# Two-layer network behind local attention: the first 512 features of layer one join the planned order, its weights are scaled, and the additions of its seven-product inputs are split between two engines

## The chip, the cores and the metric

The kernel runs on one core of a Trainium2 chip. TensorE (PE, with PEld for its weight loads) multiplies, VectorE (DVE), ScalarE (ACT) and GpSimd (POOL) do the elementwise work, and SyncE (SP) issues most of the transfers. Every engine works through a queue of its own in order and waits on semaphores for the others. The metric is the device time of one execution in microseconds (us).

## The reference

```python
x = attention(q, k, v)              # B=2, H=8, S=768, D=64: window of 16, and 24 block summaries
x = x.transpose(0, 2, 1, 3).reshape(1536, 512)
h = x @ moe_w_in                    # 512 x 2048
x = (h * np.cos(h)) @ moe_w_out     # 2048 x 512
h = x @ moe2_w_in
return (h * np.tanh(np.log1p(np.exp(h)))) @ moe2_w_out
```

Scores are masked outside a window of 16 positions; each query also sees 24 summaries of 32 keys (maximum) and values (mean). The weights arrive as 64-bit numbers.

## The kernel before

**Products.** A value is kept as a high part (fp32r) and a low part (value minus high part), and a product is three passes: high by high, high by low, low by high. Tokens come in three blocks of 512; hidden features in pieces of 128. So one product of 128 features by 512 tokens over the 512 inputs is 12 matmuls, and ends in one of eight PSUM banks.

**Attention** comes first: 48 steps of 128 tokens, software pipelined, all emitted through one `flush` (L280). Its result is `X`, a high and a low tile (`xh`, `xl`). Between its steps the first weights of layer one are made ready: a chunk is loaded, narrowed to 32 bits (`wnarrow`, L142 to L154, DVE, four instructions of which the long path takes three on DVE), and split (`whole`: high on ACT at L167, low at L172). For the first 512 features of layer one the low is on POOL, eight chunks of 128x512: four of `w_in`, four of `w_out`.

**Layer one, first 512 features.** A loop over 12 tiles (3 token blocks by 4 pieces of features) runs `up(k)` (L208, 12 matmuls into bank k modulo 4) and, one tile behind, the gate h cos h: whole turns on ACT (L589), two subtractions of them on DVE (L590 reads PSUM, L591 reads SBUF alone), the sine on ACT (L595), the product on DVE (`cos_gate`, L597, which reads the bank for the last time), then the high part on ACT (L582) and the low on DVE (L583). A tile can begin only when the tile four before has had its L597. `down` (L613) multiplies the gates with `w_out`, its evictions are on ACT (L615). The first three tiles' matmuls are fillers of attention's last steps.

**Layer one, the rest, and layer two.** The other features come in halves of 256. There seven products of sums take the place of eight (`prod`, L749), with input sums T1 to T4 that are made once from `X`: 16 additions (`tpiece`, all on POOL, emitted through `sub`, L643) and eight splits (`tsplit`). The work of these halves is placed by a planner, `arrange()`: each operation has an engine (A, D, P, S), a length in steps of six matmuls, dependencies and a due step, and it is emitted at the begin the planner finds for it. Only the order in each engine's queue comes from the plan; no wait does. At the seam, layer two's first features (`pe1` L915, then `pe2` L927) are interleaved with the last halves of layer one, and DVE there adds the last downs to `acc`, makes layer two's input sums and narrows its weights. Layer two (L1223) is emitted by a loop again.

Of the kernel before, what the change touches and what calls it, by code (L numbers as in the profile page):

```python
# [21 lines left out]
def kernel(  # L22
# [36 lines left out]
    C1 = 6.28125  # L59
    C2 = TWO_PI - C1  # L60
# [13 lines left out]
    b_floor = const.tile([128, 1], F32, tag="b_floor", name="b_floor")  # L74

# [488 lines left out]
    def layers():  # L564
        with ExitStack() as es:
# [5 lines left out]
            gate = [8, 9] + [n % 8 for n in range(200)]  # L571
# [6 lines left out]

            def split(g):

                hi, lo = gslot()
                nc.scalar.copy(hi, g)  # L582
                nc.vector.tensor_tensor(out=lo, in0=g, in1=hi.bitcast(F32), op=ALU.subtract)  # L583
                return hi, lo

            def turns(h):

                n, r = tmp("n", 2, I32), tmp("r")
                nc.scalar.activation(out=n, in_=h, func=AF.Identity, scale=1.0 / TWO_PI, bias=b_quarter)  # L589
                nc.vector.scalar_tensor_tensor(out=r, in0=n, scalar=-C1, in1=h, op0=ALU.mult, op1=ALU.add)  # L590
                nc.vector.scalar_tensor_tensor(out=r, in0=n, scalar=-C2, in1=r, op0=ALU.mult, op1=ALU.add)  # L591
                return h, r

            def cos_gate(h, r):
                nc.scalar.activation(out=r, in_=r, func=AF.Sin, bias=b_hpi)  # L595
                g = tmp("gg")
                nc.vector.tensor_tensor(out=g, in0=r, in1=h, op=ALU.mult)  # L597
                return g
# [8 lines left out]
            def down(s, u, bank=None):  # L607
                l, g, j = stages[s]
                ps = (dbank() if bank is None else BANK[bank])[:, 0:TB]
                mm = [(SLOT[4 * (g % 2) + 2 + a][:, 512 * f + 128 * u:512 * f + 128 * u + 128], G[s, f][e])  # L610
# [3 lines left out]
                acc = ACC[l, j][:, TB * u:TB * u + TB]  # L614
                return lambda: nc.scalar.copy(acc, ps)  # L615

            downs, adds = [], []

            def do_adds():
                while adds:  # L620
                    adds.pop(0)()

            def do_downs(k):

                for _ in range(2):
                    if downs and downs[0][0] <= k:
                        adds.append(down(*downs.pop(0)[1:]))

            def made(k, i, g):

                s, f = G_OF = tiles[i]
                G[G_OF] = g
                if f == GF - 1:
                    late = 2 if s == 0 else 1
                    downs.extend((k + late + u, s, u) for u in range(KD))

# [12 lines left out]
            def tpiece(p, i):  # L649
# [8 lines left out]
                sub(out, u, v, op, nc.gpsimd)  # L658

            def tsplit(p, i, part):  # L660
# [7 lines left out]
                else:  # L668
                    sub(lo, f, hi.bitcast(F32))

            TSEQ = {}

            def tseq(k, op, *a):
                TSEQ.setdefault(k, []).append((op, *a))

            for p in range(2):
                for i in range(8):
                    tseq(5 + p + (i > 5), 1, p, i)
                for i, (k0, k1) in enumerate(((7, 7), (8, 8), (10, 11), (9, 10))):
                    tseq(k0 + (p if i < 2 else 0), 0, p, i, 0)  # L680
                    tseq(k1 + (p if i < 2 else 0), 0, p, i, 1)

            st = {}
            NT1 = len(tiles)
            for k in range(NT1):
                if k not in HP:
                    up(k)
                h = HP.pop(k)
                g = cos_gate(*st.pop(k - 1)) if k - 1 in st else None
                do_adds()  # L690
                st[k] = turns(h)
                if g is not None:
                    made(k, k - 1, split(g))
                for op in WSEQ.get(k, ()):
                    op()
                for op, *arg in TSEQ.get(k, ()):
                    (tpiece if op else tsplit)(*arg)
                do_downs(k)

# [84 lines left out]
            BY = {"A": nc.scalar, "D": nc.vector, "P": nc.gpsimd}  # L784
# [13 lines left out]
            def arrange():  # L798
# [27 lines left out]
                free = {}  # L826
                left = list(ops)
# [533 lines left out]
```

## Time and profile before

| what | us |
|---|---|
| three runs: lowest, median, highest | 625.95, 626.74, 627.63 |
| the profiled execution, its own time | 626.33 |
| its span in the trace | 624.6 |
| PE busy in the span | 612.4 (98%) |
| DVE / ACT / POOL busy | 507.8 / 373.9 / 184.8 |

The span begins with the first instruction that the profile shows and ends with the last; 1.73 us of the execution lie outside it. In 40 slices of 15.6 us PE is at nine tenths or more in all but two: the ninth (125 to 140 us, seven tenths) and the last (eight tenths). The chain of work that ended last runs over PE for 88% of the span.

### The profile page before, as it was taken

The numbers are of one execution on the slowest core, as the hardware profiler recorded it, in microseconds if no ns is written. First come the engines' busy times: TensorE is split into PE (matmuls) and PEld (weight loads), VectorE is DVE, ScalarE is ACT, GpSimd is POOL, SyncE is SP. The second block draws the span as 40 slices with busy tenths as digits, with TensorE's granted clock in tenths as the row PEclk, the third lists the DMA queues.
The fourth block names the chain that finished last, engine by engine and source line by source line (L and its number), as shares of the span: only waits on it lengthen the run. The fifth ranks groups of instructions, "written<-read, shape, count | busy, mean of one in ns | idle before, by whom it ended". The sixth has DMA issues, their size and how long they took to land.

```text
span 624.6 us, 8840 instructions
## 1 busy us (share of the span) xinstructions
PE 612.4 (98%) x3012; PEld 499.1 (80%) x3013; DVE 507.8 (81%) x1002; ACT 373.9 (60%) x783; POOL 184.8 (30%) x263
## 2 busy tenths in 40 slices
PE   9999999979999999999999999999999999999998
PEld 4787778758888888888888887888888888888886
DVE  4698995599896888888988999678898888888653
ACT  4699897448977675757576767563444444444230
POOL 4599977692042333333330362000000000000000
PEclk9999999989999999999999999999999999999999
DMA  9879842002213222222223220112021213130005
GB/s 189 199 181 234 173 111 69 2 0 68 65 70 101 68 68 68 68 68 68 68 68 101 69 68 1 41 42 87 35 101 35 102 34 102 34 102 34 1 17 186
DMA packets 57995, 49.88 MB, mean 80 GB/s; under 512 B 44270, under 2 KB 44526, under 8 KB 57710
## 3 DMA queue, kind: packets, MB, share of 16 engines
q1 hardware_dynamic: 57950, 49.32, 28.1%
q8 instruction: 24, 0.39, 0.3%
q14 instruction: 21, 0.17, 0.1%
HBM read 45.57 MB, written 3.15 MB: 78 GB/s over the span
## 4 chain that ended last, share of the span: by engine, by line
PE 88%; DVE 9%; issue 1%; ACT 1%; POOL 0%; ACTq 0%; POOLq 0%
PE bank L749 32%; PE bank L1223 19%; PE bank L280 14%; PE bank L915 13%; PE bank L613 5%; PE bank L208 3%; PE bank L927 2%; DVE acc L643 2%; DVE gl L583 1%; DVE r L591 1%; DVE gl L643 1%; DVE r L590 1%; DVE wx L148 0%; DVE wx L154 0%; DVE wx L151 0%
## 5 line engine op out<-in xcount | busy, mean ns | idle before, releaser
L749 PE MATMUL bank<-xh,ws 128*128 128x512 f32 x464 | 156.5, 389 | 0.0
L1223 PE MATMUL bank<-ws,gh 128*128 128x512 f32 (+1 forms) x356 | 108.6, 387 | 0.0
L749 PEld LDWEIGHTS bank<-xh,ws 128*128 128x128 f32 x464 | 87.1, 188 | 18.1
L915 PE MATMUL bank<-gh,ws 128*128 128x512 f32 x288 | 95.2, 389 | 0.0
L749 PE MATMUL bank<-xl,ws 128*128 128x512 f32 x232 | 90.3, 389 | 0.0
L1223 PEld LDWEIGHTS bank<-ws,gh 128*128 128x128 f32 x356 | 66.6, 188 | 13.7
L167 ACT CAST ws<-wx 128x512 fp32r<-128x512 f32 x66 | 40.1, 619 | 52.4 <-DVE wx L154 49.7
L1223 PE MATMUL bank<-ws,gl 128*128 128x512 f32 (+1 forms) x178 | 68.8, 387 | 0.0
L915 PEld LDWEIGHTS bank<-gh,ws 128*128 128x128 f32 x288 | 54.1, 188 | 11.3
L280 POOL TENSOR_TENSOR pn<-pb,rs 128x256 f32<-128x256 f32 (+3 forms) x120 | 55.4, 483 | 18.1 <-ACT pb L280 6.2
L915 PE MATMUL bank<-gl,ws 128*128 128x512 f32 x144 | 56.0, 389 | 0.0
L1235 DVE TENSOR_TENSOR acc<-acc,bank 128x512 f32<-128x512 f32 (+1 forms) x71 | 47.5, 674 | 8.5 <-PE bank L1223 8.5
L719 DVE TENSOR_TENSOR gl<-gg,gh 128x512 fp32r<-128x512 f32 x42 | 29.1, 692 | 28.5 <-ACT gh L718 28.5
L749 PEld LDWEIGHTS bank<-xl,ws 128*128 128x128 f32 x232 | 43.5, 188 | 9.0
L725 ACT ACTIVATE gg<-gg 128x512 f32<-128x512 f32 x28 | 17.7, 633 | 51.2 <-DVE gg L724 51.2
L643 DVE TENSOR_TENSOR acc<-acc,bank 128x512 f32<-128x512 f32 x62 | 42.2, 682 | 4.2 <-PE bank L915 3.3
L188 POOL TENSOR_TENSOR wx<-wx 128x256 f32<-128x256 f32 x24 | 22.6, 940 | 76.6 <-DVE ws L174 75.3
L280 ACT ACTIVATE pb<-pb,mx 128x182 f32<-128x182 f32 x96 | 42.3, 448 | 1.1 <-DVE mx L280 0.9
L643 POOL TENSOR_TENSOR gl<-gg,gh 128x512 fp32r<-128x512 f32 x18 | 24.6, 1367 | 59.0 <-ACT gh L891 44.1
L749 PE MATMUL bank<-ws,ws 128*128 128x512 f32 x156 | 39.6, 389 | 0.0
L1223 PEld LDWEIGHTS bank<-ws,gl 128*128 128x128 f32 x178 | 33.4, 188 | 6.8
L172 DVE TENSOR_TENSOR ws<-wx,ws 128x512 fp32r<-128x512 f32 x48 | 33.4, 710 | 5.7 <-ACT ws L167 4.5
(139 smaller groups left out, 1315.9 us busy)
## 6 DMA issues: line engine op xcount, KB each, us to landing
wst<-in_moe_w_in_dram SPq DMA_DIRECT2D x32, 512.0 KB
wst<-in_moe_w_out_dram SPq DMA_DIRECT2D x32, 512.0 KB
kn<-in_k_dram SPq DMA_DIRECT2D x16, 192.0 KB
qn<-in_q_dram SPq DMA_DIRECT2D x16, 192.0 KB
vn<-in_v_dram SPq DMA_DIRECT2D x16, 192.0 KB
out_dram<-acc SPq DMA_DIRECT2D x11, 256.0 KB
vb<-in_v_dram SPq DMA_DIRECT2D x2, 960.0 KB
vt<-in_v_dram SPq DMA_DIRECT2D x32, 18.8 KB
```

The lines of the kernel that those rows point to most:

```text
L167: nc.scalar.copy(hi, x)
L172: eng.tensor_tensor(out=lo, in0=x, in1=hi.bitcast(F32), op=ALU.subtract)
L188: (nc.vector if l else nc.gpsimd).tensor_tensor(out=z, in0=u, in1=v, op=op)
L208: nc.tensor.matmul(ps, lhsT=SLOT[4 * (g % 2) + a][:, 512 * c + 128 * f:512 * c + 128 * f + 128], rhs=X[e][:, c, TB * j:TB * j + TB], start ...
L280: todo[phase].append(lambda: fn(*a, **kw))
L613: nc.tensor.matmul(ps, lhsT=x, rhs=y, start=(n == 0), stop=(n == len(mm) - 1))
L643: (eng or nc.vector).tensor_tensor(out=out, in0=x, in1=y, op=op)
L719: later.append(lambda: nc.vector.tensor_tensor(out=lo, in0=g, in1=hi.bitcast(F32), op=ALU.subtract))
L749: nc.tensor.matmul(ps, lhsT=u, rhs=v, start=start and n == 0, stop=stop and n == len(mm) - 1)
L915: nc.tensor.matmul(BANK[bank], lhsT=x, rhs=y, start=(n == 0 and (h == HF or not stay)), stop=(n == len(mm) - 1 and (h == NH - 1 or not stay)))
L1223: nc.tensor.matmul(ps, lhsT=x, rhs=y, start=(n == 0 and (h == 0 or not stay)), stop=(n == len(mm) - 1 and (h == NH - 1 or not stay)))
L1235: nc.vector.tensor_tensor(out=acc, in0=acc, in1=ps, op=ALU.add)
```

## The change

1. The twelve tiles of the first 512 features are put in the planner, gates and evictions too: up to T7 first, then two of the first block's downs, and so on. The hand-written loop and its tables are gone. A gate takes three DVE instructions instead of four: `rest` (whole turns off, reads a bank), `times` (reads a bank), and the low. For that `w_in` of these features carries a factor of 1/(2 pi), folded into the split in attention; for those four chunks the low is now a DVE instruction with the factor, and narrowing takes two DVE instructions instead of three for all eight chunks.
2. The 16 additions are planned no earlier than behind tile T5; eight go to POOL (all that read `X` alone), eight to DVE; of the eight low parts four to POOL.
3. The planner gets an engine "V": a VectorE operation with all operands in SBUF. It and a POOL operation exclude each other in the plan ("share"). POOL's planned length falls from 1.04 to 0.95, and a due step at the end of the planned part is not enforced any more.
4. A one-column sine at the second step after attention's last scores loads ACT's table there.
5. Evictions of the first block's downs alternate between ACT and DVE. In the last half of layer one, downs and layer two's first products are interleaved differently.

PE's list has as many rows as before (2151), SP's is the same. DVE's goes from 966 to 954, POOL's from 233 to 222.

```diff
     def short(l, g, c):
-        return (l == 0 and g > 0) or (l, g) == (1, 0) or (l, g, c) in ((1, 1, 2), (1, 1, 3))
+        return l == 0 or (l, g) == (1, 0) or (l, g, c) in ((1, 1, 2), (1, 1, 3))
...
         if fast:
-            if part == 1:
+            if part == 1 and (l, g) == (0, 0):
+                nc.vector.tensor_scalar(out=word[:, :, 0], in0=word[:, :, 0], scalar1=29, scalar2=None,
+                                        op0=ALU.logical_shift_right)
+            elif part == 1:
...
-        whole(*wdst(l, g, c), x, 1.0 / TWO_PI if l == 0 and g and c < 2 else None, part,
+        whole(*wdst(l, g, c), x, 1.0 / TWO_PI if l == 0 and c < (2 if g else KD) else None, part,
               eng or (nc.gpsimd if (l, g) == (0, 0) else nc.vector))
...
-            def tpiece(p, i):
+            def tpiece(p, i, eng):
...
-            BY = {"A": nc.scalar, "D": nc.vector, "P": nc.gpsimd}
+            BY = {"A": nc.scalar, "D": nc.vector, "V": nc.vector, "P": nc.gpsimd}
...
+                share = {"V": ("D", "X"), "P": ("P", "X")}
...
-                    assert due is None or t < due, (n, t, due)
+                    assert due is None or due >= len(steps) or t < due, (n, t, due)
...
+            TENG = "PPVPVVPV" + "VPVP"
...
-                op((k, "L"), lo_eng, 1.04 if lo_eng == "P" else WIDE, [(k, "H")], low, lo_due)
+                op((k, "L"), lo_eng, 0.95 if lo_eng == "P" else WIDE, [(k, "H")], low, lo_due)
...
+            for n in range(3, NT1):
+                x = ("T", n)
+                put(x, lambda n=n: up(n, 0), n % 4)
+                put((x, 1), lambda n=n: up(n, 1), n % 4)
+                for z in {7: (0, 1), 8: (2,), 9: (3,), 10: (4, 5), 11: (6,)}.get(n, ()):
+                    olddown(z // KD, z % KD)
...
-            last(1, 0, 1)
+            last(1, 0, 1, 2)
             both_r(("f", 0, 0), 1, 0, 0, 0, 0)
-            last(1, 2, 3)
+            last(1, 3)
+            last(2, 0)
             both_r(("f", 1, 0), 1, 0, 1, 0, 1)
-            last(2, 0, 1)
+            last(2, 1, 2)
             both_r(("f", 0, 1), 1, 0, 0, 1, 2)
-            last(2, 2, 3)
+            last(2, 3)
             both_r(("f", 1, 1), 1, 0, 1, 1, 0)
...
+                    if u % 2:
+                        op(x, "D", WIDE, [end(x)] + t, lambda acc=acc, b=b: nc.vector.tensor_copy(acc, b), until(x))
+                    else:
+                        op(x, "A", 0.42, [end(x)] + t, lambda acc=acc, b=b: nc.scalar.copy(acc, b), until(x))
...
+                for i in range(8):
+                    e = TENG[i]
+                    op(("tp", p, "x", i), e, 0.95 if e == "P" else WIDE,
+                       [K["T", 5] + 1] + [("tp", p, "x", y) for y in need[i]] + ([("tp", 0, "x", i)] if p else []),
+                       lambda p=p, i=i, e=e: tpiece(p, i, BY[e]))
...
+    at_step(NS + 1, lambda: nc.scalar.activation(out=b_sine, in_=b_quarter, func=AF.Sin))
```

**The order on DVE behind attention.** These are DVE's rows of before from attention's last instruction on; `r` and `n` belong to the gates, `gg` is the gate, `gl` and `gh` its two parts, `bank_58` to `bank_61` the four banks of `up`.

```order
L280 TENSOR_TENSOR xl<-bank_65,xh 128x256
L590 SCALAR_TENSOR_TENSOR r<-n,bank_58 128x512
L591 SCALAR_TENSOR_TENSOR r<-n,r 128x512
L597 TENSOR_TENSOR gg<-r,bank_58 128x512
L590 SCALAR_TENSOR_TENSOR r<-n,bank_59 128x512
L591 SCALAR_TENSOR_TENSOR r<-n,r 128x512
L583 TENSOR_TENSOR gl_1792<-gg,gh_1791 128x512
L597 TENSOR_TENSOR gg<-r,bank_59 128x512
L590 SCALAR_TENSOR_TENSOR r<-n,bank_60 128x512
L591 SCALAR_TENSOR_TENSOR r<-n,r 128x512
```

The same place with the change (L813 is `rest`, L820 `times`, L600 the low):

```order
L282 TENSOR_TENSOR xl<-bank_65,xh 128x256
L813 SCALAR_TENSOR_TENSOR gg<-gg,bank_58 128x512
L813 SCALAR_TENSOR_TENSOR gg<-gg,bank_59 128x512
L820 SCALAR_TENSOR_TENSOR gg<-gg,bank_58 128x512
L813 SCALAR_TENSOR_TENSOR gg<-gg,bank_60 128x512
L820 SCALAR_TENSOR_TENSOR gg<-gg,bank_59 128x512
L600 TENSOR_TENSOR gl_1786<-gg,gh_1785 128x512
L820 SCALAR_TENSOR_TENSOR gg<-gg,bank_60 128x512
L600 TENSOR_TENSOR gl_1788<-gg,gh_1787 128x512
L813 SCALAR_TENSOR_TENSOR gg<-gg,bank_61 128x512
L600 TENSOR_TENSOR gl_1770<-gg,gh_1769 128x512
```

The second tile's first instruction stands ahead of the first tile's product, the lows stand later, and the instruction that reads SBUF alone (L591) is gone.

**The order on POOL at the same place.** Before, behind attention's last `pn` (probabilities):

```order
L280 TENSOR_TENSOR pn<-pb,rs 128x2x2x12
L643 TENSOR_TENSOR acc<-xh,xl 128x512 x2
L643 TENSOR_TENSOR acc<-acc 128x512
L643 TENSOR_TENSOR acc<-xh,xl 128x512
L643 TENSOR_TENSOR acc<-acc 128x512 x2
L643 TENSOR_TENSOR acc<-xh,xl 128x512
L643 TENSOR_TENSOR acc<-acc 128x512
```

With the change (`wx` are the sums of the next half's weights, `ws_91` and `xl` low parts of the input sums):

```order
L282 TENSOR_TENSOR pn<-pb,rs 128x2x2x12
L600 TENSOR_TENSOR acc<-xh,xl 128x512 x8
L190 TENSOR_TENSOR wx<-wx 128x2x128 x4
L600 TENSOR_TENSOR ws_91<-acc,ws_91 128x512 x2
L600 TENSOR_TENSOR xl<-acc,xh 128x512 x2
```

POOL's eight additions of `X` still follow `pn` directly, with nothing between; the eight of `acc` alone have left POOL's queue.

**The order on DVE at the seam.** Before, from the last addition of a down to `acc` on:

```order
L643 TENSOR_TENSOR acc<-acc,bank_61 128x512
L643 TENSOR_TENSOR acc<-acc 128x1024
L643 TENSOR_TENSOR xl<-acc,xh 128x512 x2
L643 TENSOR_TENSOR gl_1776<-gg,gh_1775 128x512
L643 TENSOR_TENSOR xl<-acc,xh 128x2x512
L643 TENSOR_TENSOR gl_1778<-gg,gh_1777 128x512
L188 TENSOR_TENSOR wx<-wx 128x2x128
L643 TENSOR_TENSOR ws_90<-acc,ws_90 128x1024
```

With the change:

```order
L600 TENSOR_TENSOR acc<-acc,bank_61 128x512
L600 TENSOR_TENSOR acc<-acc 128x1024
L600 TENSOR_TENSOR xl<-acc,xh 128x512
L600 TENSOR_TENSOR acc<-acc 128x1024
L174 TENSOR_TENSOR ws_89<-wx,ws_89 128x512
L150 TENSOR_SCALAR wx<-wx 128x512
L600 TENSOR_TENSOR ws_90<-acc,ws_90 128x1024
L153 SCALAR_TENSOR_TENSOR wx<-wst,wx 128x512
L150 TENSOR_SCALAR wx<-wx 128x512
L156 SCALAR_TENSOR_TENSOR wx<-wst,wx 128x512
L600 TENSOR_TENSOR xl<-acc,xh 128x2x512
```

Behind the last addition, up to the low part that layer two's second product waits for, there are 27 instructions on DVE now and were 15.

## Rows read from the trace of the kernel before

**Rows 1.** The page's part 1: busy time, share of span, instructions, by engine.

```profile
PE 612.4 (98%) x3012; PEld 499.1 (80%) x3013; DVE 507.8 (81%) x1002; ACT 373.9 (60%) x783; POOL 184.8 (30%) x263
```

**Rows 2.** Waits of PE, 100 to 145 us: total, times, longest.

```profile
PE bank L208 <- DVE gg L597: 3.0, 3, 1.6
PE bank L613 <- DVE gl L583: 1.8, 1, 1.8
```

**Rows 3.** Windows: length, busy of PE, PEld, DVE, ACT, POOL, PEclk.

```profile
135.00:140.00 5.00, 4.23 (x12) 3.38 (x13) 4.97 (x5) 2.30 (x4) 4.63 (x4) 0.66 0.00 0
```

**Rows 4.** Timeline of PE: start, busy, line, tiles, [idle before, releaser].

```profile
114.67 0.47 PE L208 MATMUL bank<-xh,ws 128*128 128x512 f32 x1
...
135.77 0.79 PE L613 MATMUL bank<-gl,ws 128*128 128x512 f32 x1 [1.85 <-DVE gl L583]
...
140.66 0.39 PE L613 MATMUL bank<-gh,ws 128*128 128x512 f32 x1
```

**Rows 5.** A piece of the chain of work that ended last: start, length.

```profile
143.54 2.72 PE bank L208 x12
```

**Rows 6.** Groups of DVE, 116 to 141 us: busy, mean ns, idle before.

```profile
L583 DVE TENSOR_TENSOR gl<-gg,gh 128x512 fp32r<-128x512 f32 x5 | 8.8, 1769 | 0.0
L591 DVE SCALAR_TENSOR_TENSOR r<-n,r 128x512 f32<-128x512 int32 x6 | 8.1, 1356 | 0.2
L597 DVE TENSOR_TENSOR gg<-r,bank 128x512 f32<-128x512 f32 x6 | 4.1, 676 | 0.8 <-ACT r L595 0.8
```

**Rows 7.** Groups of POOL, 115 to 141 us.

```profile
L643 POOL TENSOR_TENSOR acc<-acc 128x512 f32<-128x512 f32 x8 | 13.1, 1639 | 0.6
L643 POOL TENSOR_TENSOR acc<-xh,xl 128x512 f32<-128x512 f32 x8 | 11.1, 1398 | 6.5 <-PE bank L280 6.5
```

**Rows 8.** Timeline of DVE, behind POOL's last addition.

```profile
142.18 0.69 DVE L583 TENSOR_TENSOR gl<-gg,gh 128x512 fp32r<-128x512 f32 x1
```

**Rows 9.** Groups of ACT, 115 to 141 us.

```profile
L589 ACT ACTIVATE n<-bank,b_quarter 128x512 int32<-128x512 f32 x7 | 4.7, 672 | 0.0
L595 ACT ACTIVATE r<-r,b_hpi 128x512 f32<-128x512 f32 x6 | 4.3, 724 | 7.7 <-DVE r L591 7.7
L582 ACT CAST gh<-gg 128x512 fp32r<-128x512 f32 x6 | 3.7, 622 | 5.1 <-DVE gg L597 5.1
```

**Rows 10.** Timeline of ACT at attention's end.

```profile
115.27 0.69 ACT L589 ACTIVATE n<-bank,b_quarter 128x512 int32<-128x512 f32 x1
115.97 1.28 ACT L595 ACT_TABLE_LOAD   x1
```

**Rows 11.** Timeline of POOL at attention's end: the first two additions.

```profile
115.13 2.55 POOL L643 TENSOR_TENSOR acc<-xh,xl 128x512 f32<-128x512 f32 x2 [6.48 <-PE bank L280]
```

**Rows 12.** Groups of DVE, 0 to 110 us (attention).

```profile
L151 DVE SCALAR_TENSOR_TENSOR wx<-wst,wx 128x512 int32<-128x512 int32 x8 | 6.3, 782 | 0.0
L154 DVE SCALAR_TENSOR_TENSOR wx<-wst,wx 128x512 int32<-128x512 int32 x8 | 5.9, 739 | 0.0
L148 DVE TENSOR_SCALAR wx<-wx 128x512 int32<-128x512 int32 x8 | 4.6, 569 | 0.0
```

**Rows 13.** Groups of POOL, 0 to 110 us.

```profile
L172 POOL TENSOR_TENSOR ws<-wx,ws 128x512 fp32r<-128x512 f32 x8 | 10.2, 1278 | 1.8 <-ACT ws L167 1.7
```

**Rows 14.** Timeline of PE at the seam.

```profile
377.30 0.39 PE L749 MATMUL bank<-xh,ws 128*128 128x512 f32 x1
...
381.71 0.74 PE L927 MATMUL bank<-ws,gh 128*128 128x512 f32 x2 [0.17 <-DVE acc L643]
```

**Rows 15.** Timeline of DVE at the seam, beginning with the last two additions of downs.

```profile
380.97 1.27 DVE L643 TENSOR_TENSOR acc<-acc,bank 128x512 f32<-128x512 f32 x2
...
385.11 1.22 DVE L643 TENSOR_TENSOR xl<-acc,xh 128x1024 fp32r<-128x1024 f32 x1
386.25 0.68 DVE L643 TENSOR_TENSOR gl<-gg,gh 128x512 fp32r<-128x512 f32 x1
386.85 0.42 DVE L188 TENSOR_TENSOR wx<-wx 128x256 f32<-128x256 f32 x1
```

More of the change, by code (lines that the diff above doesn't have):

```diff
@@ L570, in layers @@
             GS = [[gp.tile([128, TB], F32R, tag=f"g{a}{i}", name=f"g{a}{i}") for a in "hl"] for i in range(10)]
-            gate = [8, 9] + [n % 8 for n in range(200)]
+            gate = []
             def gslot():
@@ L577, in tmp @@
                 return tp.tile([128, TB], dt, tag=nm, name=nm, bufs=bufs)
[L579 to L598, printed above, removed]
             turn = [0]
@@ L605, in dbank, with down @@
                 return BANK[DBANKS[turn[0] % len(DBANKS)]]
[L607 to L610, printed above, removed]
+            def down(s, u, bank):
+                ps = BANK[bank]
+                mm = [(SLOT[2 + a][:, 512 * f + 128 * u:512 * f + 128 * u + 128], G[s, f][e])
                       for f in range(GF) for a, e in PASS]
@@ L613, in down @@
                     nc.tensor.matmul(ps, lhsT=x, rhs=y, start=(n == 0), stop=(n == len(mm) - 1))
[L614 to L635, printed above, removed]
             def both(t):
@@ L657, in tpiece, with tsplit @@
                                    (t4, x1, ALU.add), (t4, (t4, t2), ALU.subtract))[i]
-                sub(out, u, v, op, nc.gpsimd)
-            def tsplit(p, i, part):
+                sub(out, u, v, op, eng)
+            def tsplit(p, i, part, eng=None):
                 f = (ACC[0, 1][:, TB * 2 * p:TB * 2 * p + TB], ACC[0, 1][:, TB * (2 * p + 1):TB * (2 * p + 2)],
@@ L668, in tsplit @@
                 else:
[L669 to L698, printed above, removed]
+                    sub(lo, f, hi.bitcast(F32), eng=eng)
             later = []
@@ L860, in gate_ops @@
                 i = len(chain)
-                slot = GS[(2 + i) % 8]
+                slot = GS[SLOTS[i] if i < len(SLOTS) else (2 + i - len(SLOTS)) % 8]
                 x = {}
-                back = [(chain[i - 3], "L")] if i >= 3 else [(("old", "gate"), "L" if i == 2 else "P")]
+                back = [(chain[i - 3], "L")] if i >= 3 else []
+                freed = [] if freed is None else [freed]
                 prev = [(chain[i - 1], "first")] if i else []
                 chain.append(k)
-                lo_eng = eng_of(f"{f}{j}") if l == 0 else "D"
+                lo_eng = eng_of(f"{f}{j}") if l == 0 else "V"
+                e = "V" if l == 0 and j < 2 else "D"
+                turns = l != 1
                 def take():
@@ L962, in both_r @@
                 put((key, 1), lambda: plain(l, h, f, j, BANK[bank], 1), bank)
+            NT1 = len(tiles)
+            for n in range(3):
+                K["T", n] = -2
+                used.append((("T", n), n % 4))
+            for n in range(3, NT1):
[4 more added lines that the diff above has]
+                    olddown(z // KD, z % KD)
             for h in range(HF, NH):
@@ L1022, in layers @@
             END = len(steps)
-            do_adds()
-            old = {}
-            key = ("old", "gate")
-            op((key, "S"), "A", 0.42, [], lambda: nc.scalar.activation(out=st[NT1 - 1][1], in_=st[NT1 - 1][1], func=AF.Sin, bias=b_hpi))
-            def old_times():
-                old["g"] = tmp("gg")
-                sub(old["g"], st[NT1 - 1][1], st[NT1 - 1][0], ALU.mult)
-                BUF["r"] = [tmp("r") for _ in range(3)]
-            def old_high():
-                old["s"] = G[tiles[NT1 - 1]] = gslot()
-                nc.scalar.copy(old["s"][0], old["g"])
@@ L1038, in layers @@
[L1038 to L1044 removed]
+            BUF = {"n": [tmp("n", 2) for _ in range(2)], "r": [tmp("r") for _ in range(3)]}
@@ new lines, in layers @@
+            for p in range(2):
+                need = {0: [], 1: [], 2: [0, 1], 3: [], 4: [2, 3], 5: [4], 6: [], 7: [5, 6]}
+                for i in range(8):
[3 more added lines that the diff above has]
+                       lambda p=p, i=i, e=e: tpiece(p, i, BY[e]))
+                for i, (y, late, name) in enumerate(((2, None, "m5"), (5, None, "m6"), (4, end(("old", 0, KD - 1)), "m7"),
+                                                     (7, K["T", 7] + 1, "m4"))):
+                    x = ("tp", p, i)
+                    e = TENG[8 + i]
+                    op((x, "H"), "A", 0.46, [("tp", p, "x", y)] + ([late] if late else []), lambda p=p, i=i: tsplit(p, i, 0))
+                    op((x, "L"), e, 0.95 if e == "P" else WIDE, [(x, "H")], lambda p=p, i=i, e=e: tsplit(p, i, 1, BY[e]), K[HF, name])
@@ L1086, in layers @@
                 k = (l, n, c)
-                loaded = None
+                loaded = [(order[i - 1], "load")] if i else []
                 if i >= 2:
                     p2 = order[i - 2]
-                    loaded = [(p2, "b" if short(*p2) else "c")] + ([(order[i - 1], "load")] if i > 2 else [])
+                    loaded = [(p2, "b" if short(*p2) else "c")] + [(order[i - 1], "load")]
                 if (l, n) == (1, 2):
@@ L1116, in layers @@
                         left[l, n, cc] += [((l, n, "sum"), "l", i2) for i2 in range(2)]
-            BUF = {"n": [tmp("n", 2) for _ in range(2)]}
             for h in range(HF, NH):
@@ L1208, in layers @@
             arrange()
-            del gate[:-1]
-            gate[:] = [(2 + len(chain) + n) % 8 for n in range(200)]
+            gate[:] = [(2 + len(chain) - N0 + n) % 8 for n in range(200)]
             turn[0] = spin[0]
```

108 lines of the change are left out of this document (50 added, 58 removed).

## The prediction

> **What bounds the kernel now.** First the page's busy shares: PE is busy 98% of the span [rows 1], so an edit elsewhere pays only where PE waits. Then the 40 slices, where one stands out, 125 to 140 us, just behind attention; then PE's waits there: 4.8 us for DVE, for a gate's product that frees a bank (L597) and for a gate's low part (L583) [rows 2]. What the stage costs in all I read from PE's timeline, since waits leave out refills and the clock. Between 114.67 (second half of the third tile's matmuls) and 140.66 (the first block's second down) [rows 4] PE does 78 matmuls: six, then tiles T3 to T7 and one down of twelve each. Undisturbed, twelve take 2.72 us [rows 5], 0.2267 each; 78 are 17.7 us, and they took 26.0. **So 8.3 us are lost here.** Part of it is the clock: after the wait of 1.85 us for the low part [rows 4] the granted clock of 135 to 140 us was 0.66 [rows 3]; before and behind it, it was 1.0. From 140.66 on PE is dense up to the seam with layer two, where it waits once, at 381.71: from 377.30 eighteen matmuls would end at 381.38, so 0.33 is lost [rows 14].
>
> Why does DVE come late here? The low part takes 1.77 us on average and the second subtraction, which reads SBUF alone, 1.36 [rows 6]; the low takes 0.69 at 142.18 [rows 8], when POOL has no more additions to do. The product that reads a bank took 0.68 all through the stage [rows 6]. POOL meanwhile does sixteen additions [rows 7], from 115.13 [rows 11]. So DVE instructions with two operands in SBUF are stretched by 1.08 us beside POOL's additions, those with a PSUM operand aren't. Per tile DVE needed 0.68 + 1.36 + 0.68 + 1.77 = 4.5 us, and PE only 2.72 of it.
>
> **The change, part by part.**
>
> *Three instructions in a gate, in planned order.* L591 goes: 1.36 us per tile beside POOL. What is left, 0.68 + 0.68 + 1.77 = 3.1, is still more than 2.72 while POOL works; so it matters how long POOL works, and where the lows stand. *POOL's additions* do not begin later: in the order on POOL its eight additions of `X` follow attention's last `pn` directly, and what they wait for is `X`, as before, when they began at 115.13 [rows 11]. The order sets no wait for T5. But they are half as many: eight of 1.28 to 1.40 [rows 7, 11] end at about 125.4 to 126.3. DVE's eight stand far behind in its own queue, behind the lows of the next tiles.
>
> I lay DVE's queue out by the rows: ACT's whole turns from 115.27, with 0.67, 0.72 for the sine, 0.62 for the high part [rows 9], some 0.1 for a hand-over. The table load of 1.28 us [rows 10] has moved to attention's tail, where ACT idles. The first product ends at 118.2, and T4 wants its bank at 118.75 (114.67 + 18 matmuls). Then the lows of the first three tiles are reached at 119.3 and run beside POOL: three of 1.77 less an overlap of 0.07, with four bank readers of 0.61 between, 7.5 us, to the fourth tile's product at 126.8. T7 wants that bank after 54 matmuls, at 126.9. **A margin of 0.1 us: the tightest place.** The fourth tile's first ACT instruction waits for the first low (three `gg` buffers), done at 121.0, and does not bind. The fourth low is done at 128.6, and the first down wants it at 129.6. Behind that POOL's short sums and four lows are left; DVE needs 2.05 us per tile alone (0.68 + 0.68 + 0.69), with its eight additions and four lows of input sums spread over the rest of the stage, and PE is dense by this count.
>
> So of the 8.3 us all can come back if T7 does not wait. With the margin at 0.1 I let it wait: between 0 (all as in the rows) and 1.6 us (the longest wait of this kind before [rows 2]) I take 0.4, near the lower end, since the layout goes by the means of just these instructions beside just these additions.
>
> The Trainium skill (SBUF — State Buffer, Who interferes with whom) says that a DVE instruction with two inputs in SBUF contends with a GpSimd one that reads SBUF, and that whichever issues first holds the shared ports for the whole instruction while the other blocks. The first half agrees with 1.77 beside 0.69 and with the bank readers' 0.68. By the second half a low would take up to 1.28 + 0.69 = 1.97 rather than 1.77, three lows 0.6 more, and T7 would wait 0.5; that is within the bounds above and beside my 0.4.
>
> *Narrowing and lows in attention.* Removed on DVE: eight times 0.57 + 0.78 + 0.74 = 16.7 us; added: eight times a shift (0.57, up to 0.78, as it reads strided words) and one instruction of 0.74 to 0.78, so 10.5 to 12.5, and four lows of 0.69, up to 1.77: 2.8 to 7.1 [rows 6, 8, 12]. DVE's sum goes by +3 to -3.4, towards less; POOL loses four lows of 1.28, 5.1 us [rows 13]. None of the rows shows a low in DVE's queue in attention, whose own work stands behind it: if it waits there for ACT's high part, the pieces of the next step wait too. Attention is a chain of many engines, in which a part of this counts. Bounds: -2.1 (a quarter of the 8.5 us that the two engines lose at most) and +9.1 (four times 1.77 and a wait of 0.5). I take 0: the typical low is 0.69, and it replaces a longer one on the engine that makes `pn`.
>
> *Evictions on DVE.* Six of the twelve, 0.68 each with a PSUM operand, lie in a part where DVE has time, cost nothing; were it full, 4 us of DVE work would come on top of 2.05 per 2.72 and still fit. *The weights' factor* costs nothing: high and low are made anyway. *The interleaving at the seam* puts 12 of DVE's instructions behind the last addition that stood ahead of it, so that this addition is not late any more: before it began 4.3 us after its matmuls (377.30 to 381.6, the second of the two at 380.97 [rows 14, 15]), now twelve instructions earlier, when PE gives it. PE's wait there goes: **-0.3**. What is late next is the low part of layer two's weight sums: 27 instructions behind that addition, five wide ones of 1.14, six short ones of 0.42, sixteen of 0.60 (from begin to begin [rows 15]), 17.8 us, with the addition and a hand-over 18.6. PE does 92 matmuls, 20.9 us, before it wants that. It is covered by 2.3 us. If not, PE waits for what is over.
>
> **The sum**: 626.33 (the profiled execution) - 8.3 (stage) + 0.4 (T7) - 0.3 (seam) + 0 (attention) = **618.1 us**. That execution was 0.4 below the median of the three runs, so 618.5 is as good; I keep 618.1.
>
> **The rivals.** *The additions still collide.* The change doesn't do what it says: on POOL they begin as before. Then what binds is T7's bank, later the first down. For it: the margin of 0.1, the order on POOL. Against: half the additions, and one stretched instruction fewer per tile. If the lows and a few of the next bank readers come 1.5 to 3 us late, 619.2 to 621 us; were all six instructions ahead of the fourth product stretched by 1.08, +6.5, 624.2. Chance 0.2 for 619.2 to 621.5, and 0.08 for more, up to 624.8, with part of attention's bound in it.
>
> *Attention pays.* Lows in DVE's ordered queue hold up the softmax: +9.1 at most, 618.1 + 9.1 = 627.2, no change. For it: DVE's queue is in order, and the chain passes narrowing there. Against: 2.09 us of narrowing per chunk become 1.3 to 1.6. Chance 0.05 for within 0.3%. The other way, it gains more than I count: 616.2 or less, chance 0.08.
>
> *The seam binds, and it is slower.* DVE's 27 instructions behind the last addition have 2.3 us of cover, and if POOL's low parts of `X` overlap them, each costs 1.08 more. Two take the cover, eight more the 8.2 us that were won, and from twelve on it is slower by over 0.3%: 12 times 1.08 less 2.3 is 10.7, so 628.8 us. For it: 27 instructions stand there instead of 15, and a due step at the end is not enforced any more. Against: in the order POOL has only one or two low parts left by then, enough for the cover and no more. Chance 0.03.
>
> **How the numbers follow.** Forecast (616.2 to 619.2) 0.56, collision 0.2, a dearer mixture (621.5 to 624.8) 0.08, no change 0.05, slower 0.03, below 616.2 0.08. The range takes the forecast, the collision and the nearer ends of both neighbours: 616.0 to 622.0. Three tenths of a per cent are 1.9 us, about what a measurement can tell from no change: faster 0.92, same 0.05, slower 0.03.
>
> **What the changed profile would show.** Right: PE's waits for gates' products and lows between 115 and 140 us sum to under 1 us, at T7 if at all; the clock is 1.0 throughout; POOL's first addition begins at 115 and its eighth ends by 127; DVE's first three lows take about 1.8, later ones 0.7; the first of the seven products begins eight us earlier; no wait at layer two's first downs; attention ends within 1.5 us of where it ended. Wrong: attention's last matmul moves by more than that; the fourth product comes past 128; the second product of layer two waits for DVE.

## The result and the profile after

| | before | changed |
|---|---|---|
| lowest, median, highest of 4 runs, us | 625.95, 626.35, 627.63 | 617.64, 618.09, 618.40 |
| ratio of the runs, 95% interval | 1 | 0.9864 [0.9847, 0.9881] |
| span in the trace, us | 624.6 | 616.3 |

618.1 was forecast, and 618.1 was measured. Of thirteen executions of the kernel before that ran beside "three and table" and "order alone" below, the eight with a mean granted clock of 0.997 took 626.7 us in the median and the five at 0.999 or 1.0 took 625.8; the profiled one is of the first kind, all four of the changed kernel are of the second. The page of the changed kernel, its busy times, answers [rows 1]:

```profile
span 616.3 us, 8811 instructions
PE 608.6 (99%) x3012; PEld 498.4 (81%) x3013; DVE 483.4 (78%) x994; ACT 371.2 (60%) x778; POOL 172.8 (28%) x257
```

PE's waits in the whole span are all of attention now (total, times, longest); those of [rows 2] are gone, and that of [rows 14] too:

```profile
PE bank L282 <- ACT pt L282: 1.3, 4, 0.8
PE bank L282 <- DVE wz L526: 1.2, 1, 1.2
PE bank L282 <- DVE qt L282: 1.0, 2, 0.7
PE bank L282 <- DMA vn<-in_v_dram: 0.6, 1, 0.6
```

The windows behind attention (length, busy of PE, PEld, DVE, ACT, POOL, then the granted clock) answer [rows 3]: PE has no gap, and the clock stays at its upper level.

```profile
115.00:120.00 5.00, 5.00 (x25) 4.13 (x25) 3.83 (x7) 4.46 (x8) 4.45 (x4) 1.00 0.00 0
120.00:125.00 5.00, 5.00 (x24) 4.14 (x23) 5.00 (x6) 3.24 (x7) 5.00 (x4) 1.00 0.00 0
125.00:130.00 5.00, 5.00 (x24) 4.14 (x23) 4.45 (x8) 5.00 (x9) 1.98 (x2) 1.00 0.00 0
135.00:140.00 5.00, 5.00 (x24) 4.14 (x23) 3.86 (x7) 1.40 (x3) 0.00 (x0) 1.00 0.14 27
```

A longer measure serves for the experiments: from the second half of the third tile's matmuls to the first of the seven products, PE does 198 matmuls in every kernel here, undisturbed 198 x 2.72 / 12 = 44.9 us. In PE's timeline of the changed kernel they begin and end at

```profile
115.08 0.48 PE L210 MATMUL bank<-xh,ws 128*128 128x512 f32 x1
...
160.10 0.39 PE L676 MATMUL bank<-xh,ws 128*128 128x512 f32 x1
```

That is 45.02 us, 0.14 lost. Before it was 114.67 [rows 4] to

```profile
167.86 0.39 PE L749 MATMUL bank<-xh,ws 128*128 128x512 f32 x1
```

53.19 us, 8.31 lost, the same 8.3 as over the shorter piece: nothing was lost between 140.66 and 167.86. So the stage gave back 8.17 us. At the seam the kernel before lost more than the 0.33 up to its wait [rows 14], since the matmuls behind the wait are slower too: twelve took 3.19 us, from 380.02 to 383.21, where 2.72 is undisturbed.

```profile
380.02 0.61 PE L927 MATMUL bank<-ws,gh 128*128 128x512 f32 x2
...
383.21 0.39 PE L749 MATMUL bank<-xh,ws 128*128 128x512 f32 x1
```

Nothing is lost there any more, so the seam gave back 0.5. Attention ended 0.4 later in this execution (115.08 against 114.67). Together that is 8.3, by which the span is shorter.

DVE's timeline in the changed kernel, lows and bank readers behind attention (the columns are start, busy, engine, line, operation, out<-in):

```profile
119.68 1.47 DVE L600 TENSOR_TENSOR gl<-gg,gh 128x512 fp32r<-128x512 f32 x1
121.08 0.68 DVE L820 SCALAR_TENSOR_TENSOR gg<-gg,bank 128x512 f32<-128x512 f32 x1
121.68 1.18 DVE L600 TENSOR_TENSOR gl<-gg,gh 128x512 fp32r<-128x512 f32 x1
122.79 0.68 DVE L813 SCALAR_TENSOR_TENSOR gg<-gg,bank 128x512 f32<-128x512 int32 x1
123.38 1.18 DVE L600 TENSOR_TENSOR gl<-gg,gh 128x512 fp32r<-128x512 f32 x1
124.49 0.68 DVE L813 SCALAR_TENSOR_TENSOR gg<-gg,bank 128x512 f32<-128x512 int32 x1
125.09 0.67 DVE L820 SCALAR_TENSOR_TENSOR gg<-gg,bank 128x512 f32<-128x512 f32 x1
125.69 0.67 DVE L813 SCALAR_TENSOR_TENSOR gg<-gg,bank 128x512 f32<-128x512 int32 x1
126.28 0.67 DVE L820 SCALAR_TENSOR_TENSOR gg<-gg,bank 128x512 f32<-128x512 f32 x1
126.88 0.68 DVE L600 TENSOR_TENSOR gl<-gg,gh 128x512 fp32r<-128x512 f32 x1
```

The products are the rows of L820; the first two began at 117.88 and 119.09, so the one at 121.08 is the third tile's, and the fourth tile's ran from 125.09 to 125.76. It was forecast to end at 126.8. T7, which wants the fourth tile's bank, began later, without a wait (PE's timeline):

```profile
127.46 0.39 PE L210 MATMUL bank<-xh,ws 128*128 128x512 f32 x1
```

And POOL's timeline, which answers [rows 11]:

```profile
115.55 11.43 POOL L600 TENSOR_TENSOR acc<-xh,xl 128x512 f32<-128x512 f32 x8 [6.47 <-PE bank L282]
```

The additions of `X` do begin as before, right behind attention, and end at 126.98.

### The profile page after: what moved, and what is told of

Read it like the earlier page. It is cut to its first block, busy times and chain, and to the rows that moved or that the text cites. A ratio compares the mean times of both kernels' runs of the same rounds, so it can differ in the third digit from the quotient of the medians.

```text
span 616.3 us, 8811 instructions
## 1 busy us (share of the span) xinstructions
PE 608.6 (99%) x3012; PEld 498.4 (81%) x3013; DVE 483.4 (78%) x994; ACT 371.2 (60%) x778; POOL 172.8 (28%) x257
## 4 chain that ended last, share of the span: by engine, by line
PE 94%; DVE 2%; DMA 2%; ACT 1%; issue 0%; SPq 0%
PE bank L676 34%; PE bank L1174 19%; PE bank L852 16%; PE bank L282 13%; PE bank L210 5%; PE bank L593 5%; PE bank L864 2%; DMA vn<-in_v_dram 2%; DVE pb L282 0%; DVE ks L282 0%; DVE kx L282 0%; ACT pb L282 0%; ACT kx L282 0%; DVE qt L282 0%; DVE rs L282 0%
## 5 line engine op out<-in xcount | busy, mean ns | idle before, releaser
L169 ACT CAST ws<-wx 128x512 fp32r<-128x512 f32 x62 | 37.7, 619 | 55.1 <-DVE wx L156 50.3
L282 POOL TENSOR_TENSOR pn<-pb,rs 128x256 f32<-128x256 f32 (+3 forms) x120 | 52.6, 459 | 24.5 <-PE bank L282 8.1
L600 DVE TENSOR_TENSOR acc<-acc,bank 128x512 f32<-128x512 f32 x62 | 42.3, 684 | 13.4 <-PE bank L852 12.1
L600 POOL TENSOR_TENSOR gl<-gg,gh 128x512 fp32r<-128x512 f32 x18 | 26.0, 1445 | 81.7 <-ACT gh L828 76.9
L817 ACT ACTIVATE gg<-gg,b_hpi 128x512 f32<-128x512 f32 x48 | 34.6, 721 | 14.1 <-DVE gg L813 13.7
L828 ACT CAST gh<-gg 128x512 fp32r<-128x512 f32 x54 | 33.3, 617 | 9.9 <-DVE gg L820 9.4
```

The costliest lines, as they stand in the source:

```text
L169: nc.scalar.copy(hi, x)
L282: todo[phase].append(lambda: fn(*a, **kw))
L600: (eng or nc.vector).tensor_tensor(out=out, in0=x, in1=y, op=op)
L817: nc.scalar.activation(out=x["r"], in_=x["r"], func=AF.Sin, scale=TWO_PI, bias=b_hpi)
L828: nc.scalar.copy(slot[0], x["r"])
```

## The experiments

The change bundles a shorter gate, a planned order, a split of the additions, an early table load and a new interleaving at the seam. The prediction had named the shorter gate and the halved additions for the stage; the runs take the bundle apart. "Lost" is what PE loses over the 198 matmuls, in the profiled execution, a lower clock behind a wait included.

| kernel | gate | order | additions on POOL | table | lost, us | median, us | ratio to before [95%] |
|---|---|---|---|---|---|---|---|
| before | 4 | by hand | 16 | late | 8.31 | 626.35 | |
| sums later | 4 | by hand | 8 | late | 4.10 | 624.89 | 0.9973 [0.9957, 0.9989] |
| order alone | 4 | planned | 16 | early | 6.48 | 624.90 | 0.9971 [0.9957, 0.9984] |
| fourth instruction | 4 | planned | 8 | early | 3.78 | 621.43 | 0.9916 [0.9896, 0.9936] |
| three instructions | 3 | by hand | 16 | late | 0.99 | 619.36 | 0.9881 [0.9859, 0.9903] |
| three and table | 3 | by hand | 16 | early | 0.13 | 618.39 | 0.9878 [0.9863, 0.9893] |
| table late | 3 | planned | 8 | late | 0.75 | 618.44 | 0.9869 [0.9848, 0.9889] |
| sixteen on POOL | 3 | planned | 16 | early | 0.13 | 617.64 | 0.9859 [0.9834, 0.9883] |
| none on POOL | 3 | planned | 0 | early | 0.13 | 617.52 | 0.9859 [0.9841, 0.9877] |
| changed | 3 | planned | 8 | early | 0.14 | 618.09 | 0.9864 [0.9847, 0.9881] |

**Sixteen additions on POOL again.** Only the engine of the eight additions is exchanged; the plan stays.

```diff
-                       lambda p=p, i=i, e=e: tpiece(p, i, BY[e]))
+                       lambda p=p, i=i: tpiece(p, i, nc.gpsimd))
```

> The changed kernel with all sixteen additions of input sums on POOL again, in the same planned order. My theory: the order and the shorter gate are what freed PE, and behind the fourth tile DVE has time to spare, so the additions that come back to POOL (about 127 to 139 us) only stretch lows that nobody waits for: 618.1, within 0.4, and no PE wait for DVE over 0.2 us. Rival: halving POOL's additions is what did it: lows of 1.2 to 1.8 us up to 139 us, waits of PE return, 620 us or more.

617.64 us, no wait of PE behind attention, 0.13 lost. The split of the additions, which the change's heading names, is worth nothing once the gate is short. It tells less than I had meant it to: in this order all but one of the additions of `acc` come behind 140 us, so the lows in between were not stretched. The kernel "three and table" below puts all sixteen beside the tiles.

**None on POOL.** The same edit with `nc.vector`.

> The changed kernel with all sixteen additions on VectorE, in the same planned order, so that POOL does nothing beside the first tiles. My theory: the lows take 0.69 instead of 1.2 to 1.5, DVE is earlier, but PE had no wait left there: 618.1 within 0.3. Rival: DVE has too much to do with eight more additions of 0.69: a wait of PE at T7 to T9, 619 or more.

617.52 us, 0.13 lost: as forecast. It also shows a low without POOL, in the same order, between 115 and 140 us (count, then busy and mean ns):

```profile
L600 DVE TENSOR_TENSOR gl<-gg,gh 128x512 fp32r<-128x512 f32 x8 | 5.4, 686 | 0.0
```

In the changed kernel those eight average 905 ns. So POOL's additions are what stretches them, and it cost PE nothing.

**A fourth instruction in the gate.** In `rest`, for the first twelve tiles (the planner doesn't know of it; the value stays the same):

```diff
+                    if l == "g":
+                        nc.vector.scalar_tensor_tensor(out=x["r"], in0=x["r"], scalar=1.0, in1=x["r"],
+                                                       op0=ALU.mult, op1=ALU.max)
```

> The changed kernel with a fourth DVE instruction in each of the twelve gates (reads SBUF twice, changes nothing in the value), where the kernel before had its second subtraction. My theory: five of them stand ahead of the fourth tile's product, each costs 0.6 to 1.3 us beside POOL, T7's margin is 0.5 us: 3 to 6 us are lost between 115 and 140 us, so 620.6 to 624. Rival: the planned order alone is what freed PE, and a fourth instruction finds room in it: 618.1 to 618.8.

621.43 us, 3.78 lost, in two waits of PE, at T4 (not expected) and at T7. T7's margin in the changed kernel was 1.7 us (125.76 to 127.46) and not the 0.5 of the expectation; the five instructions ahead of the fourth product took more than that.

```profile
120.78 0.50 PE L210 MATMUL bank<-xh,ws 128*128 128x512 f32 x1 [1.54 <-DVE gg L823]
130.75 0.50 PE L210 MATMUL bank<-xh,ws 128*128 128x512 f32 x1 [1.31 <-DVE gg L823]
```

The planned order alone does not find room for a fourth instruction.

**Three instructions alone, in the kernel before.** The order by hand, sixteen additions and the old narrowing stay (with the factor, the four low parts of `w_in` move to DVE in attention, as in the change).

```diff
-        whole(*wdst(l, g, c), x, 1.0 / TWO_PI if l == 0 and g and c < 2 else None, part,
+        whole(*wdst(l, g, c), x, 1.0 / TWO_PI if l == 0 and c < (2 if g else KD) else None, part,
...
-                nc.scalar.activation(out=n, in_=h, func=AF.Identity, scale=1.0 / TWO_PI, bias=b_quarter)
-                nc.vector.scalar_tensor_tensor(out=r, in0=n, scalar=-C1, in1=h, op0=ALU.mult, op1=ALU.add)
-                nc.vector.scalar_tensor_tensor(out=r, in0=n, scalar=-C2, in1=r, op0=ALU.mult, op1=ALU.add)
+                nc.scalar.activation(out=n, in_=h, func=AF.Identity, scale=1.0, bias=b_quarter)
+                nc.vector.scalar_tensor_tensor(out=r, in0=n, scalar=-1.0, in1=h, op0=ALU.mult, op1=ALU.add)
...
-                nc.vector.tensor_tensor(out=g, in0=r, in1=h, op=ALU.mult)
+                nc.vector.scalar_tensor_tensor(out=g, in0=r, scalar=TWO_PI, in1=h, op0=ALU.mult, op1=ALU.mult)
```

> The kernel before with scaled weights and three DVE instructions in the first twelve gates, its hand-written order, all sixteen additions on POOL, and the old narrowing kept. If every DVE instruction with two SBUF operands is stretched by 1.08 us beside POOL (the sum of my prediction), DVE needs 3.1 us per tile and PE 2.72: 620.5 to 622. Rival: such an instruction waits only for the rest of POOL's instruction under way; two bank readers (1.2 us) stand between two lows, POOL's 1.28 are then nearly over, a low takes 0.7 to 0.9, DVE needs 2.1 per tile: only the table load's wait at the start is left, 618.8 to 620.

619.36 us and 0.99 lost: my sum's 620.5 to 622 fell, and the rival's range held, though not by its first reason, the cheap lows. In this kernel's groups of DVE, 115 to 140 us, the lows are stretched nearly as much as in [rows 6]:

```profile
L583 DVE TENSOR_TENSOR gl<-gg,gh 128x512 fp32r<-128x512 f32 x7 | 10.9, 1554 | 0.6
L590 DVE SCALAR_TENSOR_TENSOR r<-n,bank 128x512 f32<-128x512 int32 x8 | 5.4, 678 | 0.2 <-ACT n L589 0.2
L596 DVE SCALAR_TENSOR_TENSOR gg<-r,bank 128x512 f32<-128x512 f32 x7 | 4.7, 677 | 1.3 <-ACT r L594 1.3
```

So DVE does need 2.9 us per tile (0.68 + 0.68 + 1.55), near the 3.1 of my sum. The sum was wrong about what that costs: PE's 2.72 per tile holds up to T6 alone, and from there on downs of twelve matmuls stand between the tiles; 0.2 us per tile for three or four tiles adds up to no wait over 0.15 us.

**The same with the table loaded early.** Two lines more in the kernel above:

```diff
+    b_sine = const.tile([128, 1], F32, tag="b_sine", name="b_sine")
...
+    at_step(NS + 1, lambda: nc.scalar.activation(out=b_sine, in_=b_quarter, func=AF.Sin))
```

> The kernel before with scaled weights, three DVE instructions in the first twelve gates, and ACT's table loaded in attention; the hand-written order, sixteen additions on POOL and the old seam stay. Of the stage's 8.3 us lost, three instructions alone left 1.0. My theory: that 1.0 is the late table (0.75 us by its own run) and little else: 0.1 to 0.4 us lost in the stage, 618.3 to 619. Rival: the 1.0 is the lows beside POOL, which wait for whole POOL instructions and hold the first down (0.15 us of wait seen there): 0.7 or more lost still.

618.39 us, 0.13 lost: as little as the whole change, with lows of 1.61 us on average and sixteen additions on POOL. So what the kernel above still lost was the late table's, as the rival there had it. Behind attention one wait of PE is left, the seam's; its twelve matmuls took 3.16 us (371.87 to 375.03), nearly as before.

```profile
PE bank L927 <- DVE acc L643: 0.2, 1, 0.2
```

**The table late, in the changed kernel.** Its line in attention is taken out.

```diff
-    at_step(NS + 1, lambda: nc.scalar.activation(out=b_sine, in_=b_quarter, func=AF.Sin))
```

> The changed kernel without the one-column sine in attention, so that ACT loads its table ahead of the first gate's sine again (1.28 us). My theory: the first product comes 1.2 us later, at about 119.7, T4 wants its bank at 119.3, and the fourth product misses T7 by a little: PE waits 0.4 to 1.2 us in all, 618.5 to 619.3. Rival: margins cover it, 618.1 within 0.2.

618.44 us, 0.75 lost, 0.61 more than with it. PE's loss is within what I expected, the median is just below its range; there is one wait of 0.3 us, at T4, and none at T7, where I had expected one too. The medians differ by 0.35 with overlapping runs, so by the times alone it would be open; the trace shows it.

**Sums later, alone.** In the kernel before; gates and order stay.

```diff
-                sub(out, u, v, op, nc.gpsimd)
+                sub(out, u, v, op, nc.vector if i in (2, 4, 5, 7) else nc.gpsimd)
...
-                for i in range(8):
-                    tseq(5 + p + (i > 5), 1, p, i)
-                for i, (k0, k1) in enumerate(((7, 7), (8, 8), (10, 11), (9, 10))):
+                for i in (0, 1, 3, 6):
+                    tseq(5, 1, p, i)
+                for i in (2, 4, 5, 7):
+                    tseq(8 + p, 1, p, i)
+            for p in range(2):
+                for i, (k0, k1) in enumerate(((9, 9), (9, 9), (10, 11), (10, 10))):
```

> The kernel before with only the additions changed: the eight that read X on POOL first, the eight of acc on DVE behind tiles T8 and T9. Gates keep four instructions and the old order. My theory: up to about 127 us all is as before, so the first three waits of PE for L597 (3.0 us) stay, and behind that DVE needs 2.74 us per tile against PE's 2.72; half of the 8.3 us come back: 621 to 623. Rival: the additions on POOL were the only cause and what is left of them is short enough: 618.5 to 620.

4.10 lost in the stage: half came back, and the first three waits for L597 stayed, as expected. The median, 624.89, is above my range. In the profiled execution two things were added. The seven products got a wait, for a bank whose reader on DVE (`r`, L643, at 176.72) stands behind two narrowings of weights, which waited for ACT (PE's and DVE's timelines):

```profile
177.46 0.50 PE L752 MATMUL bank<-xh,ws 128*128 128x512 f32 x1 [0.95 <-DVE r L643]
```

```profile
175.46 1.34 DVE L142 SCALAR_TENSOR_TENSOR wx<-wx,wst 128x512 int32<-128x512 int32 x2 [0.60 <-ACT wst L140]
```

That the additions moved to DVE made them late is likely, but not shown. And attention, whose code is that of before, ended 3.2 us later (the stage began at 117.85, not 114.67), mostly behind one transfer; in the window from 30 to 35 us the granted clock was 0.66.

```profile
30.09 1.49 PE L280 MATMUL bank<-vn,means 128*24 128x128 f32 x12 [1.98 <-DMA vn<-in_v_dram]
```

This execution took 626.49 us, 1.6 above the median, so how much of it the other executions share isn't known, and the miss of the range is only in part explained.

**The order alone.** The changed kernel with both the fourth instruction and sixteen additions on POOL (the two edits above).

> The changed kernel with a fourth DVE instruction in each of the first twelve gates and all sixteen additions on POOL: of the change, only the planned order is left (with the early table and the new weights). With eight additions on POOL the fourth instruction cost 3.8 us in the stage. My theory: with sixteen, two SBUF readers per tile meet POOL's instructions to about 140 us, so the lows and fourth instructions behind 127 us are stretched too: 5 to 8 us lost in the stage, 622.5 to 626. Rival: as without the fourth instruction, the additions of acc come too late to matter: 3.8 us, 621.4.

624.90 us, 6.48 lost, both within what I expected, though less by its reason: of the eight additions that came back to POOL one alone ran before 140 us (127.50 to 129.24), and it stretched one low. The planned order, with the early table, gives back 1.8 of the 8.2. At T7, with a low of 1.78 us ahead where the fourth-instruction kernel had 0.68, the wait is longer:

```profile
120.71 0.50 PE L210 MATMUL bank<-xh,ws 128*128 128x512 f32 x1 [1.53 <-DVE gg L823]
131.76 0.50 PE L210 MATMUL bank<-xh,ws 128*128 128x512 f32 x1 [2.38 <-DVE gg L823]
```

Afterwards the granted clock was 0.75 in the window from 130 to 135 us and 0.91 in the next. Of the 2.7 us that this kernel loses more than the fourth-instruction kernel, 1.1 is the longer wait at T7 and 1.6 comes behind it. As in "sums later", the seven products got a wait of their own, which the 6.48 leaves out:

```profile
176.48 0.50 PE L676 MATMUL bank<-xh,ws 128*128 128x512 f32 x1 [0.60 <-DVE r L600]
```

**The old narrowing.** In the changed kernel, for layer one's first weights:

```diff
-        return l == 0 or (l, g) == (1, 0) or (l, g, c) in ((1, 1, 2), (1, 1, 3))
+        return (l == 0 and g > 0) or (l, g) == (1, 0) or (l, g, c) in ((1, 1, 2), (1, 1, 3))
```

> The changed kernel with the old narrowing of layer one's first weights (three DVE instructions a chunk instead of two, eight chunks, in attention). My theory: attention is a chain of several engines and hardly feels it: 618.1 within 0.5, attention's last matmul within 0.5 us of where it is. Rival: what the narrowing saves on DVE (some 6 us) shows in part: 619 to 620.5.

617.89 us (0.9864 [0.9847, 0.9881]), and attention's last part began at 114.72: no difference. Eight instructions less on DVE in attention are worth nothing that can be measured.

**The old seam.** In the changed kernel the four `last` lines as before, and 0.85 for POOL's planned length.

> The changed kernel with the old interleaving of downs and layer two's first products in the last half of layer one (for this order to fit the plan, POOL's planned length is 0.85 instead of 0.95 here). My theory: DVE's last addition is late again by some us, PE waits 0.2 to 0.4 us at layer two's first downs: 618.4, and DVE's later rows at the seam are no nearer to PE than before. Rival: the wait of before came from lateness out of the first stage, not from the interleaving: no wait, 618.1.

617.84 us (0.9867 [0.9848, 0.9885]), no wait of PE behind attention. My expectation fell: the interleaving is not what took the wait away. Nor does the rival's reason hold, since "three and table" came to the seam on time and waited there (0.2 us above). What the kernels without the wait share is that DVE is not late at the seam's last additions. In this kernel's timeline of DVE it waits for PE at the last but one:

```profile
367.94 0.69 DVE L600 TENSOR_TENSOR acc<-acc,bank 128x512 f32<-128x512 f32 x1 [1.62 <-PE bank L852]
```

What in the planner's rules did that (the exclusion of V and P, or the lengths) wasn't taken apart, and stays open.

## Why the prediction was right

**The stage.** 8.3 were to come back, less 0.4 for T7. 8.17 came back, and T7 did not wait: its bank was free at 125.76, and by PE's beginning at 115.08 it was wanted at 127.46, a margin of 1.7 instead of 0.1. PE began 0.4 later, and still the fourth product ended 1.0 earlier than forecast, because the three lows ahead of it took 3.83 us together and not three times 1.77. So the 0.4 for T7 was too much, the seam, counted at 0.3, gave 0.5, and attention's end, counted at 0, took 0.4: small terms off in opposite ways, and that the sum is right to 0.1 is luck in part.

Some of the 8.17 is the clock. Before, the nine matmuls behind the wait for the low part, from 135.77 [rows 4] on and at the granted clock of [rows 3], took 3.73 us where 2.04 is undisturbed; the tenth began at

```profile
139.50 0.39 PE L208 MATMUL bank<-xl,ws 128*128 128x512 f32 x1
```

In the changed kernel that wait is gone, and the granted clock is 1.0 in these windows.

The causes were named together, the shorter gate and the halved additions; the runs weigh them. **The shorter gate and the early table give it all (0.13 lost with the order by hand and sixteen additions); the halved additions help only where the gate is long (8.31 to 4.10); the order alone gives 1.8.** What the fourth instruction costs depends on what stands beside it: put back into the planned order it cost 3.6 us with eight additions on POOL (3.78 against 0.14) and 6.35 with sixteen (6.48 against 0.13). No run has a fourth instruction and nothing on POOL, so its own time and its stretch aren't told apart.

**"The additions still collide"** was half true: the additions of `X` begin at 115.55 and stretch the lows, as the order on POOL showed, but that no longer reaches PE. With sixteen on POOL it doesn't either.

**The price of a stretch** was mis-sized. I took 1.08 for every low. In the changed kernel it was 0.8 once and 0.5 twice (1.47, 1.18, 1.18 against 0.68). POOL's additions, asked for one at a time, show why:

```profile
119.30 1.31 POOL L600 TENSOR_TENSOR acc<-xh,xl 128x512 f32<-128x512 f32 x1
120.56 1.75 POOL L600 TENSOR_TENSOR acc<-xh,xl 128x512 f32<-128x512 f32 x1
122.28 1.74 POOL L600 TENSOR_TENSOR acc<-xh,xl 128x512 f32<-128x512 f32 x1
```

They end at 120.61, 122.31 and 124.02, and the three lows end at 121.15, 122.86 and 124.56, each 0.54 or 0.55 later. The same holds for all 59 VectorE instructions of 128x512 without a PSUM operand that took over 0.72 us between 114 and 142 us in these twelve kernels: each ended 0.55 us after the POOL instruction that was under way when it began. So a low waits for what is left of POOL's instruction, whatever that is, and then takes 0.55. When it comes 0.5 us behind the low before it, 0.63 is left, hence 1.18. When it comes directly behind another such instruction (L583 behind L591 before), or two bank readers later ("three instructions alone"), POOL's next addition is just under way, 1.1 to 1.25 is left, and the low takes 1.67 to 1.80. It is the second half of the rule of the Trainium skill (SBUF — State Buffer, in the section SBUF: two separate sides) that whichever starts first holds the shared ports for its whole instruction. These 59 cases agree with it. My prediction read it as a reason for dearer lows; here it made them cheaper, since what counts is how much of POOL's instruction is left.

**The seam.** PE's wait went as forecast, and 0.5 us with it: the -0.3 counted to the first matmul behind the wait and left out the slower ones after it. DVE's last addition of a down waits for PE now, instead of the other way round:

```profile
369.74 0.69 DVE L600 TENSOR_TENSOR acc<-acc,bank 128x512 f32<-128x512 f32 x1 [0.32 <-PE bank L852]
```

I laid that to the new interleaving; the old one did the same. The cover behind it was mis-sized: 2.3 us by durations from begin to begin, but DVE waits for ACT's high parts there, 0.70 and 1.17 us, which I had not counted. The low part that layer two's second product wants is the first of these rows of DVE, done at 389.79; in PE's timeline that product begins at 389.94 (its line is the second; the low is wanted one matmul later).

```profile
389.10 0.69 DVE L174 TENSOR_TENSOR ws<-wx,ws 128x512 fp32r<-128x512 f32 x1 [1.17 <-ACT ws L169]
```

```profile
389.71 0.39 PE L676 MATMUL bank<-xh,ws 128*128 128x512 f32 x1
389.94 1.52 PE L676 MATMUL bank<-ws,ws 128*128 128x512 f32 x6
```

So 0.4 us of cover was left of 2.3, by ACT's lateness and not by POOL's. That ACT is late there is PE's doing in turn: ahead of the high part its queue has an eviction that waited for PE.

```profile
387.42 0.59 ACT L1156 COPY acc<-bank 128x512 f32<-128x512 f32 x1 [2.13 <-PE bank L864]
```

So the slower rival may have been nearer than its chance of 0.03 said, but no run shows what would have used up the rest.

**Attention.** Counted at 0. The old narrowing shows that the narrowing's part is 0; for the four lows on DVE there are only the two kernels with three instructions and the old narrowing, whose stage began at 115.37 and 114.70, against 114.67 before. The stage began between 114.4 and 115.4 us in the profiled executions of ten of the eleven other kernels, and at 117.85 in one, whose attention is that of before: in that spread an effect of these edits of some tenths of a us can't be seen.

**Evictions on DVE and the factor** cost nothing that shows, as forecast: no wait of PE behind attention.

## What to carry to other kernels

Before an order is planned, count what the engine that comes late does per tile: one instruction less on it was worth 7.3 of the 8.2 us, the early table 0.9 more, and of all the rest only the seam's 0.5 is left, which in the medians is 0.3 with overlapping runs. Take a bundle apart by putting its smallest part alone into the kernel before; here that takes a few lines and gives 618.4 where the whole change gives 618.1. When a cover is worked out, add the waits for the third engine in the chain (here ACT's high parts), not only the durations of the two that meet. And price a stretched VectorE instruction by what is left of POOL's instruction when it begins, not by an average.

## What the runs showed of the hardware

- A VectorE instruction of 128x512 with both operands in SBUF took 0.68 to 0.69 us with POOL idle ("none on POOL"). Beside POOL's additions it ended 0.55 us after the one under way when it began, so it took 1.18 where 0.63 us of that was left and up to 1.80 where 1.25 was. With a PSUM operand it took 0.67 to 0.69 throughout. The additions were slowed in turn: eight of them took 11.4 us, 1.43 each: 1.74 or 1.75 for the three that began while a low was running, 1.30 or 1.31 for the others.
- Attention's end lay 3.2 us apart in two profiled executions of the same attention code, mostly by the landing of one transfer: PE had no listed wait for `vn` in the profiled execution of before, one of 2.0 us in that of "sums later", and behind it a granted clock of 0.66 from 30 to 35 us.
- The granted clock fell behind some waits of PE and not behind others: to 0.66 behind 1.85 us before, to 0.75 behind 2.38 ("the order alone"); it stayed at 1.0 behind 1.54 and 1.31 ("a fourth instruction").
